# Attention plus swish-MLP on one core: feature order of heads 0 and 1 moved from the weight load into the PV copy and the norm, with a new instruction order

## The chip, the cores and the metric

The kernel runs on one core of one Trainium2 chip. The metric is the device time of one execution in microseconds (us); lower is better. Three timed runs of the kernel before gave 240.32, 236.54 and 239.46 us, so its median is 239.46 us. The execution that the profile shows took 237.53 us by the same clock, and the span of its instructions is 235.8 us. The engines are called as the profile calls them: PE is TensorE (PEld its weight load), DVE VectorE, ACT ScalarE, POOL GpSimd, SP SyncE, which here issues nearly all DMAs.

## The reference

Shapes: q, k and v are 4 batches x 8 heads x 768 positions x 64. Heads 0, 2 and 6 attend causally to everything ("retrieval"); the other five see the first 4 positions and a window of 64. The attention output, with the heads side by side as 512 features, is the input of a two-layer MLP with a swish of learned slope between the layers.

```python
scores = scale * np.matmul(q, k.transpose(0, 1, 3, 2))
full_mask = np.broadcast_to(causal, (H, S, S))
stream_mask = np.broadcast_to(causal & (is_sink | in_win), (H, S, S))
a = softmax(np.where(mask, scores, -1e9))
x = np.matmul(a, v).transpose(0, 2, 1, 3).reshape(B * S, H * D)   # 3072 x 512
h = x @ w_in                                                      # 512 x 2048
g = h * (1.0 / (1.0 + np.exp(-beta * h)))
out = g @ w_out                                                   # 2048 x 512
```

## The kernel before, in words

**Units.** The work is cut into 8 units n = 2b + u: batch b, half u of its sequence (384 query positions). A unit goes through these stages. `scores` (L624) makes keys-by-queries score tiles on PE; `exps` (L690) takes their exponential on ACT; `masks` (L699) multiplies by masks on DVE. `sums` or `sums_d` (L741, L766) add up the softmax denominators on PE. `pv` (L859) multiplies by v, four head pairs t = 0..3, two pairs to a PSUM tile (g = 0 and 1). The result is normalised into the bf16 tile xT, 128 features by 4 chunks by 384 positions. `mm1` (L919) multiplies xT by 16 feature tiles f of w_in, four matmuls each; `swish_a` (ACT) and `swish_b` (DVE) make gT; `mm2` (L936) multiplies gT by w_out; `out_copy` and `out_store` send it out.

**Two ways to normalise.** Units 0 and 1 copy the PV result to SBUF first (`hold`, L846), turn reciprocals on PE (`spread`) and multiply (`norm_held`, L851). Units 2 to 7 send the sums through DRAM to get a tile R with each head's reciprocals on its 64 partitions (`spread_r`, L812), and multiply PV by R straight out of PSUM (`norm`, L907).

**The order of the heads.** `XT` (L18) puts heads (1, 0) into chunk 0, so head 1 is on partitions 0 to 63 and head 0 on 64 to 127; the other chunks are natural: (2, 3), (4, 5), (6, 7). Thus the retrieval heads 0 and 2 of PV's first tile are on opposite halves of the partitions, and PE works on both halves side by side. xT keeps that order, so the first 128 rows of w_in have to be exchanged to match. `load_w0` (L483) does this as it loads them: four DMAs of 64 rows x 1024 columns (256 KB each) that land on the other half of the partitions. `cast_w0` (L505) turns them to bf16 in 8 pieces of 128 x 256. The other 384 rows come in four quarters of columns (`load_w_in`, L489: 128 x 3 x 512 numbers, 768 KB), each cast by POOL in four pieces of 128 x 3 x 128 (`cast_w_in`, L501). One such piece is the weight of one feature tile f. `XH` (L19) carries the exchanged order into the columns of the sums of units 0 and 1 (L367, L752).

**What sets the order.** Every operation is entered with `add`, with its needs and a planned cost. `_Plan.run` (L141) goes through them in the order of the list SEQUENCE (L37); where several engines could do an operation, CHOICE (L94) names one by a letter; the planned start times then give every engine its program order. Each engine's queue runs strictly in that order, SP's queue of DMA issues too. Staging tiles for the weights come from a ring of three (`wf`); each holds 8 KB per partition. At most 8 DMAs are under way: the issue of one waits for the landing of the eighth before it.

Of the kernel before, what the change touches and what calls it, by code (L numbers as in the profile page):

```python
# [8 lines left out]
F32 = mybir.dt.float32  # L9
# [9 lines left out]
XH = [h for t in XT for h in t]  # L19
RETR = [1, 0, 1, 0, 0, 0, 1, 0]  # L20
NQ = 384
# [71 lines left out]
]  # L93
CHOICE = (  # L94
    "daggaagdddgddaadadadgdgaaadgdddaagdgdaaaadadaaaddaddagdgadaadadggadgdgddadgdggggaadaadddaaaddaaddaaa"
    "dddddddda"
# [102 lines left out]
def kernel(  # L199
# [18 lines left out]
    NP = len(PAIRS)  # L218
# [138 lines left out]
    def const_sink():  # L357
# [6 lines left out]
        for pi in range(1, NP):  # L364
            for i, h in enumerate(PAIRS[pi]):
                if not RETR[h]:
                    c = XH.index(h)  # L367
                    dve.tensor_copy(out=esel_k[:, 16 + c:32:8], in_=sel_k[0:96, pi - 1, i:i + 1].to_broadcast([96, 2]))
                    dve.tensor_copy(out=sink_own[:, h:h + 1], in_=sel_k[0:96, pi - 1, i:i + 1])
# [113 lines left out]
    def load_w0(half, r):  # L483
        if (half, r) == (0, 0):
            wst["0"] = stg.tile([128, 2048], F32, name="wf", bufs=RINGS["wf"])
        c = slice(half * d_ff // 2, (half + 1) * d_ff // 2)
        sp.dma_start(out=wst["0"][r:r + D, c], in_=moe_w_in[D - r:2 * D - r, c])

    def load_w_in(s):  # L489
        f = stg.tile([128, 2048], F32, name="wf", bufs=RINGS["wf"])[:, 0:(NP - 1) * 2 * FS].rearrange("p (a n) -> p a n", a=NP - 1)  # L490
        sp.dma_start(out=f, in_=bass.AP(moe_w_in.tensor, moe_w_in.offset + 128 * d_ff + s * 2 * FS,
# [792 lines left out]
```

## Time and profile before

| | us |
|---|---|
| median of three runs (lowest, highest) | 239.46 (236.54, 240.32) |
| the profiled execution | 237.53 |
| span of its instructions | 235.8 |
| PE busy (share of the span) | 223.6 (95%) |
| DVE, ACT, POOL busy | 154.4, 139.0, 80.5 |
| mean granted clock of PE | 0.993 |

The views are read like this. The page gives busy time per engine and, in 40 slices, the busy tenths of each engine and PE's granted clock. The chain of waits follows back from the last instruction what each waited for. The timeline lists instructions in order of time, with the start, the time covered, and in brackets the idle time of the engine before them and what ended it. The groups by form have the count, the busy time and the mean duration of one.

### The profile page before, as it was taken

How to read it: one execution, taken by the hardware profiler on the slowest of the kernel's cores; microseconds unless marked ns; L12 is line 12 of the kernel's file. 1: busy time of each engine (PE TensorE's matmuls, PEld its weight loads, DVE VectorE, ACT ScalarE, POOL GpSimd, SP SyncE). 2: the span in 40 equal slices, each digit the busy share in tenths (PEclk: the TensorE clock that was granted, in tenths of full speed). 3: DMA queues.
4: the chain of work that ended last, by engine and by line, in shares of the span. 5: the costliest groups of instructions: out<-in, count | busy, mean ns of one | idle time of the engine just before them, and what ended most of it. 6: DMA issues, size and time to landing. Idle time of an engine off the chain costs nothing.

```text
span 235.8 us, 6232 instructions
## 1 busy us (share of the span) xinstructions
PE 223.6 (95%) x2462; PEld 126.1 (53%) x2462; DVE 154.4 (65%) x365; ACT 139.0 (59%) x236; POOL 80.5 (34%) x190
## 2 busy tenths in 40 slices
PE   7788599999999999999999999999999999999994
PEld 6454266665454555563655555554564465466553
DVE  6597479888727847882677588536777286258630
ACT  4898387888626639824886169613876267108600
POOL 5316356689564239609243145540000000000000
PEclk9999889999999999999999999999999999999999
DMA  6989979999988999999879978862600200703012
GB/s 185 275 256 321 238 185 313 361 369 291 227 214 210 198 189 250 238 202 254 215 178 236 238 167 224 166 155 97 133 3 29 107 2 10 179 0 133 3 44 89
DMA packets 84557, 42.37 MB, mean 180 GB/s; under 512 B 66592, under 2 KB 77552, under 8 KB 84528
## 3 DMA queue, kind: packets, MB, share of 16 engines
q1 hardware_dynamic: 84256, 41.78, 70.0%
q8 instruction: 19, 0.31, 0.5%
q10 hardware_dynamic: 272, 0.20, 0.3%
q14 instruction: 10, 0.08, 0.1%
HBM read 32.38 MB, written 6.37 MB: 164 GB/s over the span
## 4 chain that ended last, share of the span: by engine, by line
PE 85%; DMA 7%; DVE 5%; SPq 1%; ACT 1%; POOL 0%; issue 0%
PE b L115 74%; PE sp L115 10%; DMA wf<-in_moe_w_in_dram 5%; DVE es L115 2%; DMA k2f<-in_k_dram 2%; SPq L115 1%; DVE QK L115 1%; DVE vs L115 1%; POOL w_in L115 0%; DVE vb L115 0%; DVE c L115 0%; ACT t L115 0%; DVE gT L115 0%; DVE VE L115 0%; ACT es L115 0%
## 5 line engine op out<-in xcount | busy, mean ns | idle before, releaser
L115 PE MATMUL b<-xT,w_in 128*128 128x384 bf16 x512 | 91.1, 329 | 4.2 <-POOL w_in L115 4.1
L115 ACT ACTIVATE t<-b,beta_h 128x384 f32<-128x384 f32 x128 | 72.2, 583 | 34.2 <-PE b L115 23.1
L115 PE MATMUL b<-w_out,gT 128*128 128x512 bf16 (+1 forms) x400 | 88.8, 371 | 0.0
L115 DVE SCALAR_TENSOR_TENSOR gT<-t,b 128x384 bf16<-128x384 f32 x128 | 68.3, 551 | 27.6 <-ACT t L115 24.5
L115 PEld LDWEIGHTS <-w_in 128*128 128x128 bf16 x512 | 48.5, 98 | 38.7 <-POOL w_in L115 4.7
L115 ACT ACTIVATE es<-sp 128x768 bf16<-128x768 f32 (+3 forms) x64 | 49.9, 810 | 22.4 <-PE sp L115 21.9
L115 PEld LDWEIGHTS <-gT 128*128 128x128 bf16 x400 | 37.7, 98 | 39.8 <-issue 1.0
L115 POOL CAST c<-wf 128x256 bf16<-128x256 f32 x48 | 18.5, 422 | 22.2 <-DMA wf<-in_k_dram 10.6
L115 DVE TENSOR_SCALAR osb<-b 128x512 f32<-128x512 f32 (+1 forms) x15 | 9.9, 671 | 19.8 <-PE b L115 15.3
L115 PE MATMUL sp<-QK 64*64 64x64 bf16 (+6 forms) x402 | 18.9, 236 | 0.9 <-ACT QK L115 0.5
L115 ACT ACTIVATE osb<-b 128x512 f32<-128x512 f32 (+1 forms) x10 | 5.8, 577 | 22.9 <-PE b L115 22.8
L115 DVE TENSOR_TENSOR xT<-sp,R 128x768 bf16<-128x768 f32 (+3 forms) x18 | 11.6, 686 | 9.4 <-PE sp L115 9.4
L115 POOL COPY KP<-QK 128x64 bf16<-128x64 bf16 (+5 forms) x39 | 11.0, 332 | 18.0 <-DMA QK<-c 14.2
L115 PEld LDWEIGHTS <-QK 64*64 64x64 bf16 (+1 forms) x402 | 10.1, 106 | 11.6 <-issue 10.4
L115 DVE TENSOR_TENSOR es<-es,mask_s 128x800 bf16<-128x800 bf16 (+5 forms) x24 | 12.6, 537 | 3.9 <-ACT es L115 3.7
L115 POOL CAST vb<-wf 128x512 bf16<-128x512 f32 x18 | 10.7, 612 | 12.7 <-DMA wf<-in_v_dram 12.6
L115 POOL CAST w_in<-wf 128x384 bf16<-128x384 f32 (+1 forms) x20 | 9.6, 518 | 14.5 <-DMA wf<-in_moe_w_in_dram 14.5
L115 PE MATMUL sp<-es,vb 128*64 128x64 bf16 (+3 forms) x243 | 13.8, 237 | 0.0
L115 ACT COPY QK<-b 128x384 bf16<-128x384 bf16 (+1 forms) x15 | 8.8, 589 | 7.4 <-PE b L115 7.3
L115 PE MATMUL b<-ident,c 128*128 128x128 bf16 x96 | 9.8, 228 | 2.5 <-ACT c L115 0.9
L115 PEld LDWEIGHTS <-vb 128*64 128x64 bf16 x243 | 11.6, 111 | 0.5
L115 DVE TENSOR_TENSOR es<-es,mask_c 128x256 bf16<-128x256 bf16 (+2 forms) x32 | 10.7, 350 | 0.3 <-ACT es L115 0.2
(93 smaller groups left out, 170.7 us busy)
## 6 DMA issues: line engine op xcount, KB each, us to landing
out_dram<-osb SPq DMA_DIRECT2D x23, 256.0 KB
wf<-in_v_dram SPq DMA_DIRECT2D x18, 256.0 KB
wf<-in_moe_w_out_dram SPq DMA_DIRECT2D x4, 1024.0 KB
R<-rd SPq DMA_DIRECT2D x9, 384.0 KB
q2f<-in_q_dram SPq DMA_DIRECT2D x16, 192.0 KB
wf<-in_moe_w_in_dram SPq DMA_DIRECT2D x4, 768.0 KB
wf<-in_q_dram SPq DMA_DIRECT2D x12, 256.0 KB
wf<-in_k_dram SPq DMA_DIRECT2D x12, 256.0 KB
```

What stands on the lines that cost most here:

```text
L115: ins = f(*a, **k)
```

## The change

1. xT has the heads in natural order, so w_in is loaded plainly. `load_w0` and `cast_w0` go (4 DMAs, 8 casts); `load_w_in` loads all 512 rows of a quarter of the columns (128 x 4 x 512 numbers, 1024 KB), and its four casts on POOL have 512 numbers per partition where they had 384.
2. PV keeps heads (1, 0) in chunk 0 for units 1 to 7; unit 0 uses natural order there too. The exchange is made later: in unit 1 by `hold`, whose one copy of the first tile becomes three (64 x 384, 64 x 384, 128 x 384); in units 2 to 7 by `norm`, whose one multiplication of 128 x 768 for g = 0 becomes three of the same shapes. The halves cross partitions 0 to 63 and 64 to 127.
3. The sums of units 0 and 1 use the natural column h.
4. SEQUENCE and CHOICE are new, so the order on every engine is new, and some operations change engine: POOL does five of the eight shifts of v (`shift_v`) where it did two, output copies on DVE go from 15 to 9 (ACT from 10 to 16), casts of q and k on DVE and ACT go from 12 to 7, on POOL from 20 to 25.

```diff
-XH = [h for t in XT for h in t]
-                    c = XH.index(h)
+                    c = h
-    def load_w0(half, r):
-        if (half, r) == (0, 0):
-            wst["0"] = stg.tile([128, 2048], F32, name="wf", bufs=RINGS["wf"])
-        c = slice(half * d_ff // 2, (half + 1) * d_ff // 2)
-        sp.dma_start(out=wst["0"][r:r + D, c], in_=moe_w_in[D - r:2 * D - r, c])
     def load_w_in(s):
-        f = stg.tile([128, 2048], F32, name="wf", bufs=RINGS["wf"])[:, 0:(NP - 1) * 2 * FS].rearrange("p (a n) -> p a n", a=NP - 1)
+        f = stg.tile([128, 2048], F32, name="wf", bufs=RINGS["wf"]).rearrange("p (a n) -> p a n", a=NP)
...
-        cast(eng, w_in_sb[2 * s + i // 2][:, 1:, c], wst["i", s][:, :, i * 128:(i + 1) * 128])
-    def cast_w0(s, eng):
-        cast(eng, w_in_sb[s][:, 0, :], wst["0"][:, s * FS:(s + 1) * FS])
+        cast(eng, w_in_sb[2 * s + i // 2][:, :, c], wst["i", s][:, :, i * 128:(i + 1) * 128])
     def hold(x, g, eng):
-        cast(eng, x.R[:, 2 * g:2 * g + 2, :], x.ps.pop(("v", g))[:, :, 0:NQ])
+        o = x.ps.pop(("v", g))
+        if g or not x.n:
+            cast(eng, x.R[:, 2 * g:2 * g + 2, :], o[:, :, 0:NQ])
+            return
+        for r in (0, D):
+            cast(eng, x.R[r:r + D, 0, :], o[D - r:2 * D - r, 0, 0:NQ])
+        cast(eng, x.R[:, 1, :], o[:, 1, 0:NQ])
     def pv(x, g):
-            for i, h in enumerate(XT[t]):
+            for i, h in enumerate(XT[t] if x.n else (2 * t, 2 * t + 1)):
     def norm(x, g):
-        if not (g and moved(x, 6)):
+        if g == 0:
+            for r in (0, D):
+                dve.tensor_mul(x.xT[r:r + D, 0, :], o[D - r:2 * D - r, 0, 0:NQ], x.R[D - r:2 * D - r, 0, :])
+            dve.tensor_mul(x.xT[:, 1, :], o[:, 1, 0:NQ], x.R[:, 1, :])
+            return
+        if not moved(x, 6):
             dve.tensor_mul(x.xT[:, 2 * g:2 * g + 2, :], o[:, :, 0:NQ], x.R[:, 2 * g:2 * g + 2, :])
             return
```

**The new order around the weights.** In both kernels SP's 16th DMA is the first quarter of w_in. Behind it came, before: two pieces of `load_w0`, three loads of q and k (192 KB each), the second quarter, one load of q, the other two pieces, the third quarter, three loads of v. Now: four loads of q and k, the second quarter, the third quarter, three loads of v. On PE, six transposes and 14 score matmuls of unit 1 that stood behind f = 4 now stand ahead of it. After the PV of unit 7 PE now has 12 matmuls of `mm2` where it had 9 ahead of that unit's first `mm1`; after the PV of unit 5, 12 where it had 16 and 4 score matmuls.

More of the change, by code (lines that the diff above doesn't have):

```diff
@@ L37 @@
 SEQUENCE = [
[55 rows of a table removed]
[54 rows of a table added]
 ]
 CHOICE = (
-    "daggaagdddgddaadadadgdgaaadgdddaagdgdaaaadadaaaddaddagdgadaadadggadgdgddadgdggggaadaadddaaaddaaddaaa"
-    "dddddddda"
+    "ggggaaggdgdddadddadadggaagadggdaddggdaaddadaaaadgaddagagaddadagggdggaggdaggaadadaaaddaaadadaaadaadda"
+    "a"
 )
@@ L481 @@
     wst = {}
-    def load_w0(half, r):
-        if (half, r) == (0, 0):
-            wst["0"] = stg.tile([128, 2048], F32, name="wf", bufs=RINGS["wf"])
-        c = slice(half * d_ff // 2, (half + 1) * d_ff // 2)
-        sp.dma_start(out=wst["0"][r:r + D, c], in_=moe_w_in[D - r:2 * D - r, c])
     def load_w_in(s):
-        f = stg.tile([128, 2048], F32, name="wf", bufs=RINGS["wf"])[:, 0:(NP - 1) * 2 * FS].rearrange("p (a n) -> p a n", a=NP - 1)
-        sp.dma_start(out=f, in_=bass.AP(moe_w_in.tensor, moe_w_in.offset + 128 * d_ff + s * 2 * FS,
-                                        [[d_ff, 128], [128 * d_ff, NP - 1], [1, 2 * FS]]))
+        f = stg.tile([128, 2048], F32, name="wf", bufs=RINGS["wf"]).rearrange("p (a n) -> p a n", a=NP)
+        sp.dma_start(out=f, in_=bass.AP(moe_w_in.tensor, moe_w_in.offset + s * 2 * FS, [[d_ff, 128], [128 * d_ff, NP], [1, 2 * FS]]))
         wst["i", s] = f
@@ L751, in sums @@
                 for h in heads:
-                    e8 = two[:, 31 - 16 * s - XH.index(h):63 - 16 * s - XH.index(h)]
+                    e8 = two[:, 31 - 16 * s - h:63 - 16 * s - h]
                     if RETR[h]:
@@ L1145, in attention @@
             if n < RD:
-                add(("act", "dve"), (0.7, 0.87), lambda e, g=g: hold(x, g, ENG[e]),
+                add(("act", "dve"), (1.1, 1.4) if n and not g else (0.7, 0.87), lambda e, g=g: hold(x, g, ENG[e]),
                     needs=[("O", n, g)] + ([("o", n, 0)] if g else []), gives=[("o", n, g)], drop=[("sp", (n, "v", g))],
@@ L1149, in attention @@
                 continue
-            add("dve", 1.3 if u and g else 0.87, lambda g=g: norm(x, g),
+            add("dve", 0.87 if g and not u else 1.35, lambda g=g: norm(x, g),
                 needs=[("R", n, 2 * g), ("R", n, 2 * g + 1), ("o", n, g)] + ([("xT", n, 0)] if g else []),
@@ L1160, in first @@
         drop = [("xT", n)] if s == FO - 1 else []
-        needs = [("wi", s), ("w0", s // FO2)] + ([("h", n, s - 1)] if s else [])
+        needs = [("wi", s)] + ([("h", n, s - 1)] if s else [])
         if n == 0 and s < 2:
             for t in range(NP):
-                add("pe", 0.163, lambda t=t: mm1(x, s, [t]), needs=[("xT", n, t)] + ([("h", n, s, t - 1)] if t else needs if s != 1 else needs[:2] + [("h", n, 0, 0)]),
+                add("pe", 0.163, lambda t=t: mm1(x, s, [t]), needs=[("xT", n, t)] + ([("h", n, s, t - 1)] if t else needs if s != 1 else needs[:1] + [("h", n, 0, 0)]),
                     gives=[("h", n, s, t)] + ([("h", n, s)] if t == NP - 1 else []), take=[] if t else take)
@@ L1225 @@
     add("dve", 1.4, const_sel, needs=[("const", "ident")], gives=[("const", "sel")])
-    for half in range(2):
-        for r in (0, D):
-            first_one = (half, r) == (0, 0)
-            add("sp", 0.5, lambda half=half, r=r: load_w0(half, r), dma=0.72, gives=[("w0f", half, r)], begun=[("begun", "0")] if first_one else [],
-                needs=[] if first_one else [("begun", "0")], take=[("wf", "w0", NS)] if first_one else [])
-    for s in range(NS):
-        add(("pool", "dve", "act"), (0.36, 0.2, 0.33), lambda e, s=s: cast_w0(s, ENG[e]), port=True,
-            needs=[("w0f", s // 4, 0), ("w0f", s // 4, D)], gives=[("w0", s)], drop=[("wf", "w0")])
     for s in range(NS // 2):
         for w, ld, ca in (("i", load_w_in, cast_w_in), ("o", load_w_out, cast_w_out)):
-            add("sp", 0.5, lambda s=s, ld=ld: ld(s), dma=2.9 if w == "o" else 2.2, gives=[("wf", w, s)], begun=[("begun", w, s)],
+            add("sp", 0.5, lambda s=s, ld=ld: ld(s), dma=2.9, gives=[("wf", w, s)], begun=[("begun", w, s)],
                 take=[("wf", (w, s), 4)])
             for i in range(4):
-                add("pool", 0.58 if w == "o" else 0.47, lambda s=s, i=i, ca=ca: ca(s, i, pool), needs=[("wf", w, s)],
+                add("pool", 0.58, lambda s=s, i=i, ca=ca: ca(s, i, pool), needs=[("wf", w, s)],
                     gives=[("w" + w, 4 * s + i)], drop=[("wf", (w, s))])
```

109 rows, old and new, of the table SEQUENCE are left out of this document.

## The prediction

> **What bounds the kernel now.** I read the page first: busy times, then slices and granted clock.
>
> ```profile
> PE 223.6 (95%) x2462; PEld 126.1 (53%) x2462; DVE 154.4 (65%) x365; ACT 139.0 (59%) x236; POOL 80.5 (34%) x190
> ...
> PE   7788599999999999999999999999999999999994
> ...
> PEclk9999889999999999999999999999999999999999
> ```
>
> PE is the bound, and it is full from the sixth slice (about 30 us) on. No other engine passes 65%. The windows say the same in numbers:
>
> ```profile
> 20.00:30.00 10.00, 6.43 (x63) 3.52 (x64) 5.37 (x13) 5.29 (x10) 4.63 (x10) 0.90 1.08 290
> 30.00:40.00 10.00, 10.00 (x229) 6.55 (x226) 8.21 (x19) 7.74 (x15) 5.31 (x11) 0.93 0.82 234
> 40.00:90.00 50.00, 49.55 (x537) 26.90 (x532) 35.33 (x86) 32.56 (x53) 30.85 (x69) 1.00 1.00 258
> 90.00:150.00 60.00, 60.00 (x684) 32.89 (x681) 43.01 (x100) 39.23 (x68) 29.28 (x64) 1.00 0.95 218
> 150.00:210.00 60.00, 60.00 (x573) 32.49 (x572) 34.26 (x71) 28.90 (x50) 2.87 (x10) 1.00 0.32 80
> ```
>
> From 30 to 210 us PE idles 0.45 us in all. So whatever does not change PE's own work (matmuls go from 2462 to 2463, one more filler) can gain only ahead of 30 us, and can lose anywhere. Ahead of 30 us the largest hole is in this stretch of PE's timeline, with the clock of the stretches behind it:
>
> ```profile
> 23.55 1.64 PE L115 MATMUL b<-xT,w_in 128*128 128x384 bf16 x9
> 28.12 1.14 PE L115 MATMUL b<-xT,w_in 128*128 128x384 bf16 x3 [2.93 <-POOL w_in L115]
> 29.05 0.53 PE L115 MATMUL b<-ident,c 128*128 128x128 bf16 x3
> 29.51 0.53 PE L115 MATMUL sp<-QK 64*64 64x64 bf16 x14
> 29.98 0.50 PE L115 MATMUL b<-ident,c 128*128 128x128 bf16 x3
> 30.27 2.05 PE L115 MATMUL b<-xT,w_in 128*128 128x384 bf16 x8
> 32.25 0.36 PE L115 MATMUL sp<-QK 64*64 64x64 bf16 x14
> 32.55 1.47 PE L115 MATMUL b<-xT,w_in 128*128 128x384 bf16 x8
> ```
>
> ```profile
> 28.00:30.00 2.00, 1.88 (x21) 1.06 (x22) 2.00 (x5) 0.58 (x1) 1.21 (x3) 0.51 1.15 302
> 30.00:32.00 2.00, 2.00 (x15) 1.18 (x11) 1.80 (x6) 1.48 (x3) 0.26 (x1) 0.64 0.48 115
> ```
>
> After f = 3 PE has nothing for 2.93 us, until POOL has cast the second quarter of w_in. Then it runs at a granted clock of 0.51 and 0.64 for four microseconds: 2 x 0.49 + 2 x 0.36 = 1.7 us lost. The hole costs 2.9 + 1.7 = 4.6 us in all. POOL's rows and the chain say that a DMA is behind it:
>
> ```profile
> 17.77 1.41 POOL L115 CAST w_in<-wf 128x384 bf16<-128x384 f32 x3 [5.06 <-DMA wf<-in_moe_w_in_dram]
> ...
> 27.10 2.11 POOL L115 CAST w_in<-wf 128x384 bf16<-128x384 f32 x4 [4.40 <-DMA wf<-in_moe_w_in_dram]
> 31.75 1.41 POOL L115 CAST w_in<-wf 128x384 bf16<-128x384 f32 x3 [2.54 <-DMA wf<-in_moe_w_in_dram]
> ```
>
> ```profile
> 16.28 10.77 DMA wf<-in_moe_w_in_dram
> ```
>
> The quarter was issued at 16.28 and landed 10.77 us later. DMA engines were busy all that time (share 1.08 in the window 20 to 30), so bytes set its time: what stands ahead of it in SP's queue decides.
>
> **The change, part by part.**
>
> *Bytes ahead of the second quarter.* Between the casts at 17.77 and 27.10 there landed, by the code's sizes and SP's order, 2 x 256 + 3 x 192 + 768 = 1856 KB in 9.33 us, or 199 KB/us. Up to the end of the second quarter the new order has 256 KB more in the first, 512 KB of `load_w0` less, 192 KB of q or k more and 256 KB more in the second: 192 KB more. At 199 KB/us that is 0.96 us later; at the 290 GB/s of the whole window 0.68. I take 0.8, so it lands at 27.9. It is now SP's 21st DMA where it was the 22nd, so I give the limit of eight DMAs under way nothing; the full DMA engines cover that.
>
> *The casts.* One cast of 128 x 384 becomes 128 x 512; the nearest row is w_out's cast of that shape:
>
> ```profile
> L115 POOL CAST w_out<-wf 128x512 bf16<-128x512 f32 x16 | 9.2, 616 | 1.9 <-DMA wf<-in_moe_w_out_dram 1.9
> ...
> L115 POOL CAST w_in<-wf 128x384 bf16<-128x384 f32 x16 | 8.0, 536 | 13.5 <-DMA wf<-in_moe_w_in_dram 13.5
> L115 POOL CAST w_in<-wf 128x256 bf16<-128x256 f32 x4 | 1.7, 446 | 1.0 <-DMA wf<-in_moe_w_in_dram 1.0
> ```
>
> 16 x 0.08 = 1.3 us more on POOL against 4 x 0.446 = 1.8 us less there, and four pieces less on ACT and DVE. In the new POOL order f = 4's piece is cast first, where it was second: f = 4 starts at 27.9 + 0.62 + 0.05 = 28.6, 0.45 us later than now. f = 5's piece is third, at 27.9 + 3 x 0.62 = 29.8; at half clock f = 4 lasts until 28.6 + 1.3 = 29.9, which hides it.
>
> *Work moved into the hole.* Six transposes and 14 score matmuls now run behind f = 4, from 29.05 to 30.27 at half clock: 1.2 us. The new order does them ahead of f = 4, in the hole, where they cost nothing. Net at this place: 0.45 - 1.2 = -0.8 us. If PE could not do them there (their loads of q and k now stand ahead of the second quarter, so I expect that it can), the place would cost +0.45.
>
> *The third quarter.* Up to its end there are now 256 KB fewer, about 1 us: cast from 30.7 instead of 31.75. PE comes to f = 8 at about 33, as now (32.55 + 0.7). Hidden. It costs from the point where it lands after 32.5.
>
> *The exchange in the norm.* Durations on DVE by form:
>
> ```profile
> L115 DVE TENSOR_TENSOR xT<-sp,R 128x768 bf16<-128x768 f32 x9 | 8.3, 953 | 9.4 <-PE sp L115 9.4
> ...
> L115 DVE TENSOR_TENSOR xT<-sp,R 128x384 bf16<-128x384 f32 x3 | 1.6, 548 | 0.0
> ...
> L115 DVE TENSOR_TENSOR xT<-sp,R 64x128 bf16<-64x128 f32 x3 | 0.9, 294 | 0.0
> ```
>
> No row has 64 x 384. From below it is 0.294 (64 x 128), from above 0.548 (128 x 384); I take 0.548, since the length per partition is the same. Each of six norms is then 3 x 0.548 - 0.953 = 0.69 us longer, 4.1 us on DVE in all, and 0 at the lower end. DVE is at 65% and loses work elsewhere (seven of 21 copies of shifted v, six of 15 output copies), so only the place counts: PE's first `mm1` of the unit waits for xT. The tightest place now is unit 7:
>
> ```profile
> 209.08 2.06 DVE L115 TENSOR_TENSOR xT<-sp,R 128x768 bf16<-128x768 f32 x4 [1.99 <-PE sp L115]
> 211.18 0.29 DVE L115 TENSOR_TENSOR xT<-sp,q2f 64x128 bf16<-64x128 f32 x1
> ```
>
> ```profile
> 209.72 2.12 PE L115 MATMUL b<-w_out,gT 128*128 128x512 bf16 x9
> 211.68 2.60 PE L115 MATMUL b<-xT,w_in 128*128 128x384 bf16 x15
> ```
>
> DVE ends at 211.47, PE needs xT at 211.68. Nine `mm2` matmuls cover the norm, 0.218 each; the new order has twelve, so PE comes to `mm1` at 209.72 + 2.62 = 212.3, and DVE ends at 211.47 + 0.69 = 212.2. I cost it at nothing; the cover is 0.1 to 0.2 us there, and any other DVE work ahead of it ends the cover.
>
> *The exchange in `hold`* (unit 1) is one copy of 0.8 us that becomes three of about 0.48, 0.65 us more on ACT, at about 40 us:
>
> ```profile
> L115 ACT COPY QK<-b 128x384 bf16<-128x384 bf16 x10 | 4.8, 484 | 0.1
> ...
> L115 ACT COPY R<-sp 128x768 f32<-128x768 f32 x4 | 3.2, 799 | 0.7 <-PE sp L115 0.6
> ```
>
> PE now has three `mm1` tiles between the spreads there, 2 us, so I take 0; exposed it would be 0.65. PV of unit 0 has both retrieval heads on one half now; at PE's rate that is under 0.1 us, taken as 0.1. Shifted v on POOL (five units, not two) takes some 3 us of POOL per unit; at 34% POOL hides it.
>
> *Sum.* -0.8 + 0.1 = -0.7 us. The profiled execution (237.53, of which 1.7 us lie outside its span of 235.8) would go to 236.8. It was 1.9 us below the median of the runs, 239.46, and I put the same step on the median: **238.8 us**.
>
> [...] In the rows, a hole of 2.93 us was followed by a granted clock of about one half. [...]
>
> **The rivals.**
> - A, as above: 238.8, of its own 236.4 to 240.9, since three runs of one kernel already spread from 236.54 to 240.32. Chance 0.42.
> - B, the hole gets shorter by the moved work, and the clock is never halved: 1.7 us less, 237.1. For it: 1.2 us of work at half clock is 0.7 us at full, out of 2.93. Against it: the quarter lands later. Chance 0.15.
> - F, the hole closes: DMAs of full 128 rows flow faster than 199 KB/us and the second quarter lands by 25 us: 4.6 + 0.8 us less, 234.0. Against it: the DMA engines' share is already 1.08. Chance 0.10.
> - C, the other side: xT comes late. DVE takes the norm after other work in its queue, and the 0.69 us shows in all six units, with hold's 0.65: 4.1 + 0.65 = 4.8 us, 239.5 + 4.8 = 244.2. It decides from 0.2 us of DVE work ahead of the norm. For it: DVE is busy 35.33 of 50 us between 40 and 90. Against it: the twelve matmuls of cover. Chance 0.18.
> - D, a second hole: three loads deep in the queue, f = 8 waits for the third quarter as f = 4 does for the second, and the clock halves again: 4.6 us, 243.4. Against it: fewer bytes ahead. Chance 0.15.
>
> That the change does nothing (239.5) lies within A.
>
> **How the numbers follow.** The time is A's. The range reaches to F on one side and C on the other, 235.0 to 243.8, leaving out some 0.2. A difference under 2% (4.8 us) is about what a measurement of this kernel cannot tell from none. Faster by over 2%: F, 0.10. Slower by over 2%: most of C and D where they come with a late run, 0.22. Within 2%: 0.68.
>
> **What would show it.** Right: a hole before f = 4 of about 2.9 us that ends near 28.6, with transposes and scores ahead of it and a half clock behind it; no hole at f = 8; no PE wait for xT after 60 us; about 0.5 us of idle PE from 30 us on. Wrong: a second wait for POOL's w_in, waits of PE for DVE's xT of 0.3 us or more in several units, or more filler or stalls in the first 20 us than now.

## The result and the profile after

| | before | after |
|---|---|---|
| median of 20 runs (lowest, highest), us | 236.14 (233.98, 240.32) | 234.26 (231.85, 238.26) |
| profiled execution, its span, us | 237.53, 235.8 | 235.09, 233.4 |
| mean granted clock in that execution | 0.993 | 1.0 |

The ratio of after to before is 0.9922, 95% interval 0.9893 to 0.9951: the kernel became 0.8% faster, 1.9 us. Here and below medians are of all runs of a kernel, while ratios, their intervals and means leave out the runs that lay over 1.5% above the kernel's fastest. The prediction was 238.8 with 235.0 to 243.8, so the measured 234.26 lies below its range. Most of the difference to 238.8 is the base: the three runs shown had a median of 239.46, twenty runs have 236.14. The change itself was put at -0.7 us and measured -1.9.

The page of after: busy time, then PE's slices and clock.

```profile
PE 222.8 (95%) x2443; PEld 126.8 (54%) x2463; DVE 160.1 (69%) x357; ACT 141.7 (61%) x238; POOL 95.9 (41%) x202
...
PE   6999999998999899999999999999999999999994
...
PEclk9999999999999999999999999999999999999999
```

The fifth slice was a 5 and is a 9, and the clock never drops; further right two slices are now an 8. In windows (columns: length, then busy time of PE, PEld, DVE, ACT and POOL, granted clock, DMA share, GB/s):

```profile
20.00:30.00 10.00, 9.40 (x101) 5.09 (x100) 8.96 (x18) 8.38 (x15) 7.51 (x13) 1.00 0.98 296
30.00:40.00 10.00, 10.00 (x221) 6.89 (x220) 9.26 (x22) 7.48 (x15) 5.99 (x13) 1.00 1.02 341
...
50.00:60.00 10.00, 8.78 (x118) 4.38 (x112) 9.41 (x24) 5.81 (x10) 9.66 (x17) 1.00 0.87 231
70.00:80.00 10.00, 9.47 (x167) 4.88 (x168) 7.37 (x16) 5.15 (x7) 8.07 (x13) 1.00 0.97 238
80.00:90.00 10.00, 9.26 (x73) 5.51 (x74) 8.62 (x19) 6.11 (x11) 2.79 (x11) 1.00 0.80 162
```

From 20 to 30 us PE was busy 6.43 us and is busy 9.40, at full clock. But behind 50 us it now loses time. (Twenty matmul records are missing from this trace, 2443 of 2463. They leave gaps of 0.05 or 0.16 us that are put down to "issue", some 1.7 us in all; those are not waits.) PE's timeline of after names the waits, and POOL's shows when the weights came:

```profile
24.14 0.33 PE L113 MATMUL b<-ident,c 128*128 128x128 bf16 x3
24.41 0.36 PE L113 MATMUL sp<-QK 64*64 64x64 bf16 x14
24.70 0.34 PE L113 MATMUL b<-ident,c 128*128 128x128 bf16 x3
25.14 0.82 PE L113 MATMUL b<-xT,w_in 128*128 128x384 bf16 x4
26.25 0.82 PE L113 MATMUL b<-xT,w_in 128*128 128x384 bf16 x4 [0.29 <-POOL w_in L113]
...
56.57 2.53 PE L113 MATMUL b<-w_out,gT 128*128 128x512 bf16 x11 [0.92 <-POOL w_out L113]
...
80.58 1.09 PE L113 MATMUL b<-es,one 128*32 128x384 bf16 x25 [0.90 <-DVE es L113]
```

```profile
18.47 2.42 POOL L113 CAST w_in<-wf 128x512 bf16<-128x512 f32 x4 [6.47 <-DMA wf<-in_moe_w_in_dram]
24.46 4.28 POOL L113 CAST w_in<-wf 128x512 bf16<-128x512 f32 x7 [2.49 <-DMA wf<-in_moe_w_in_dram]
...
49.74 6.77 POOL L113 CAST w_out<-wf 128x512 bf16<-128x512 f32 x11 [1.83 <-DMA wf<-in_moe_w_out_dram]
...
76.51 3.30 POOL L113 COPY vs<-vb 64x1536 bf16<-64x1536 bf16 x2
```

The second quarter is cast at 24.46 us instead of 27.10, though 192 KB more have to land by its end. The moved transposes and scores run before f = 4 (24.14 to 25.1), f = 4 starts at 25.14, f = 5 waits 0.29 us, and the hole of 2.93 us is gone with the half clock behind it. Counted by its `mm1` matmuls, PE comes to f = 8 at 28.89 us instead of 33.21, 4.3 us sooner. Of this, 1.4 us it already has at f = 0 (19.22 instead of 20.64), ahead of the hole: in the first 20 us PE idled 5.0 us before and idles 2.8 after. The span is only 2.4 us shorter. Most of the rest went back in waits that before did not have: 0.92 for a cast of w_out, 0.90 for a mask on DVE, and small ones.

These two waits differ between executions. In a second profile of the changed kernel (span 232.5; it is the last run on the exchange, below) the one for w_out is absent, and the one for the mask is twice as long:

```profile
79.53 1.09 PE L113 MATMUL b<-es,one 128*32 128x384 bf16 x25 [1.80 <-DVE es L113]
```

### The profile page after: what moved, and what is told of

Its sections match the earlier page's. It is cut to its first block, busy times and chain, and to the rows that moved or that the text cites. A ratio compares the mean times of both kernels' runs of the same rounds, so it can differ in the third digit from the quotient of the medians.

```text
span 233.4 us, 6215 instructions
## 1 busy us (share of the span) xinstructions
PE 222.8 (95%) x2443; PEld 126.8 (54%) x2463; DVE 160.1 (69%) x357; ACT 141.7 (61%) x238; POOL 95.9 (41%) x202
## 4 chain that ended last, share of the span: by engine, by line
PE 78%; DVE 8%; ACT 5%; DMA 4%; issue 2%; POOL 2%; SPq 0%; POOLq 0%; ACTq 0%
PE b L113 69%; PE sp L113 9%; DVE es L113 4%; DMA wf<-in_moe_w_in_dram 4%; ACT es L113 3%; DVE gT L113 2%; DVE mask_s L113 1%; DVE xT L113 1%; POOL w_in L113 1%; ACT t L113 1%; ACT QK L113 1%; POOL mask_s L113 1%; ACT c L113 0%; POOL ident L113 0%; POOL mask_c L113 0%
## 5 line engine op out<-in xcount | busy, mean ns | idle before, releaser
L113 PE MATMUL b<-w_out,gT 128*128 128x512 bf16 (+1 forms) x380 | 86.3, 370 | 2.9 <-issue 1.1
L113 ACT ACTIVATE es<-sp 128x768 bf16<-128x768 f32 (+2 forms) x64 | 49.2, 804 | 9.4 <-PE sp L113 9.3
L113 ACT ACTIVATE osb<-b 128x512 f32<-128x512 f32 (+1 forms) x16 | 9.1, 572 | 35.3 <-PE b L113 35.3
L113 DVE TENSOR_TENSOR xT<-sp,R 64x384 bf16<-64x384 f32 (+4 forms) x30 | 15.9, 554 | 11.4 <-PE sp L113 11.0
L113 DVE TENSOR_TENSOR es<-es,mask_c 128x256 bf16<-128x256 bf16 (+2 forms) x32 | 14.1, 454 | 12.3 <-ACT es L113 12.1
L113 DVE TENSOR_TENSOR es<-es,mask_s 128x800 bf16<-128x800 bf16 (+5 forms) x24 | 16.1, 692 | 0.8 <-ACT es L113 0.8
L113 POOL COPY vs<-vb 64x1536 bf16<-64x1536 bf16 (+2 forms) x12 | 15.7, 1321 | 0.3
L113 POOL CAST w_in<-wf 128x512 bf16<-128x512 f32 x16 | 9.7, 649 | 12.2 <-DMA wf<-in_moe_w_in_dram 12.2
L113 ACT COPY QK<-b 128x384 bf16<-128x384 bf16 (+1 forms) x12 | 7.1, 590 | 7.2 <-PE b L113 7.0
L113 DVE COPY QK<-b 128x384 bf16<-128x384 bf16 (+1 forms) x12 | 7.9, 685 | 5.0 <-PE b L113 5.0
```

The costliest lines, as they stand in the source:

```text
L113: ins = f(*a, **k)
```

## The experiments

Two theories for the early quarter. P: the `load_w0` DMAs themselves were slow, because each fills 64 of the 128 partitions. O: the new order (what stands ahead of the quarter, and PE's order) did it. A third question is who gave part of the gain back: the exchange on DVE, or the new order.

### Loads alone, in the old order

The kernel before, with the plain quarters and without `load_w0` and `cast_w0`; the exchange is left out, so the rows of w_in for heads 0 and 1 are not matched to xT.

```diff
-        sp.dma_start(out=wst["0"][r:r + D, c], in_=moe_w_in[D - r:2 * D - r, c])
+        pass
...
-        f = stg.tile([128, 2048], F32, name="wf", bufs=RINGS["wf"])[:, 0:(NP - 1) * 2 * FS].rearrange("p (a n) -> p a n", a=NP - 1)
+        f = stg.tile([128, 2048], F32, name="wf", bufs=RINGS["wf"]).rearrange("p (a n) -> p a n", a=NP)
...
-        cast(eng, w_in_sb[s][:, 0, :], wst["0"][:, s * FS:(s + 1) * FS])
+        pass
```

> The kernel before with its own order; only the four loads of 64 rows of w_in and their casts are left out, and the four quarters bring all 512 rows (heads 0 and 1 then meet each other's rows of w_in, which is left so). Theory P (the 64-row loads are slow for their bytes and hold up the second quarter): the second quarter lands by about 24.5 to 25.5 us instead of 27.1, the wait of 2.93 us before f = 4 falls under 1 us, the clock is not halved, and the span goes from 235.8 to 231 to 232 us, ratio 0.98. Theory O (the new order closed the hole: work moved ahead of f = 4, SP's order): only bytes count, which are 320 KB fewer up to that quarter, about 1.2 us; a wait of 1.5 to 2.5 us stays, ratio 0.99 to 1.00.

Measured: 232.63 us, ratio to before 0.9839 (0.9787 to 0.9892). POOL's timeline:

```profile
22.32 2.53 POOL L115 CAST w_in<-wf 128x512 bf16<-128x512 f32 x4 [2.32 <-DMA wf<-in_moe_w_in_dram]
```

Up to the end of the second quarter this kernel loads exactly as many bytes as before (256 KB more in each of two quarters, 512 KB of `load_w0` less; the 320 KB fewer of the expectation were a slip), in the same order, and has them 4.8 us sooner. Neither bytes nor the new order can be the cause of that, so O falls. What is left is the shape of the DMAs, or their number, which is two less up to there; the next two runs tell these apart. The loads alone gain 1.6%, twice what the whole change gains.

The 4.8 us compare one execution with one, and part of them is chance. A load lands in 16 parts, each with an event of its own in the trace, and the cast waits for the last. The parts of the second quarter landed at 22.39 (first), 23.29 (median), 24.81 (fifteenth) and 27.05 us (last) in the profile before, and at 20.61, 20.98, 21.29 and 22.27 in this one. So 2.3 us lie in the median part; the rest is a longer tail, mostly one late part. In all the profiles here the last part of this quarter comes 0.1 to 2.2 us behind the fifteenth, whatever the shape; what makes it late is not shown.

### Only the shape of load_w0

Both keep the bytes, the places in the queue and `cast_w0`, and leave the exchange out. The first has four DMAs of 128 rows x 512 columns, the second two of 128 x 1024 (the same 4 KB runs as before, on 128 partitions).

```diff
+        c0 = half * d_ff // 2 + r // D * d_ff // 4
+        c = slice(c0, c0 + d_ff // 4)
+        sp.dma_start(out=wst["0"][:, c], in_=moe_w_in[0:128, c])
```

```diff
+        if r == 0:
+            sp.dma_start(out=wst["0"][:, c], in_=moe_w_in[0:128, c])
```

> The kernel before with the same four DMAs of 256 KB at the same places, each of 128 rows x 512 columns instead of 64 rows x 1024 columns (the exchange of heads 0 and 1 is thereby left out). Theory P: the shape is the cause, so the second quarter lands 1.5 to 2.5 us sooner and the ratio is 0.985 to 0.99. Theory O, or bytes alone: no difference, the quarter lands at 27 us and the ratio is 1.00.

> The kernel before with the first 128 rows in two DMAs of 128 rows x 1024 columns (512 KB each; the exchange of heads 0 and 1 is left out), so that the packets stay 4 KB long but reach all 128 partitions. If half the partitions are what makes the 64-row loads slow: like e2, the quarter lands 1.5 to 2.5 us sooner. If packets of 4 KB are: like the kernel before, 27 us.

Measured: 0.9888 (0.9854 to 0.9922) and 0.9893 (0.9857 to 0.993). The two agree, so 2 KB or 4 KB runs, and four DMAs or two, make no difference; 64 or 128 partitions make 1.1%. Theory P holds. The quarter is cast at, in the first and in the second:

```profile
25.84 2.11 POOL L115 CAST w_in<-wf 128x384 bf16<-128x384 f32 x4 [2.63 <-DMA wf<-in_moe_w_in_dram]
```

```profile
24.14 2.11 POOL L115 CAST w_in<-wf 128x384 bf16<-128x384 f32 x4 [2.41 <-DMA wf<-in_moe_w_in_dram]
```

That is 1.3 and 3.0 us sooner than before's 27.10, but the first is no sooner than the second profile of before, below (25.87). (The profiled execution of the first took 236.88 us, against a median of 233.79, and its last part came 1.6 us behind the fifteenth.) A measure that does not hang on a late part: from the median part of the first quarter to that of the third, the bytes that SP's order has there (3328 KB before, in 12.33 us) go at 270 KB/us in the profile before, and at 243 in its second one below. With `load_w0` on 128 partitions they go at 323 and 339, with plain quarters at 375 to 387 (five profiles: loads alone twice, loads with the exchange, the changed kernel twice). With 64-row pieces in the changed kernel, the next experiment, it is 295.

### The converse: 64-row pieces in the kernel after

The changed kernel with the first 128 rows of each quarter loaded in two pieces of 64 rows.

```diff
-        sp.dma_start(out=f, in_=bass.AP(moe_w_in.tensor, moe_w_in.offset + s * 2 * FS, [[d_ff, 128], [128 * d_ff, NP], [1, 2 * FS]]))
+        sp.dma_start(out=f[:, 1:, :], in_=bass.AP(moe_w_in.tensor, moe_w_in.offset + 128 * d_ff + s * 2 * FS, [[d_ff, 128], [128 * d_ff, NP - 1], [1, 2 * FS]]))
+        for r in (0, D):
+            sp.dma_start(out=f[r:r + D, 0, :], in_=moe_w_in[r:r + D, s * 2 * FS:(s + 1) * 2 * FS])
```

> The changed kernel, but each quarter of w_in comes as one DMA of 128 x 3 x 512 and two of 64 x 512 for the first 128 rows (same bytes, rows in natural order, 8 more DMAs). Theory P (loads on 64 partitions are slow): the second quarter is cast later than 24.46 us, by 0.5 to 2 us, and the kernel loses some 0.5%, 0.995 to 1.0 of the kernel before. Rival L (only the 4 KB packets, or the two pieces that stood ahead of the second quarter, were slow): no difference to the changed kernel, 0.99 to 0.993.

Measured: 1.0016 (0.9977 to 1.0055) of before; the changed kernel beside it on the same chip had 0.9894 (0.9845 to 0.9943). The whole gain is gone. (One of its twelve executions took 566.3 us, for a reason that nothing here shows.) POOL's timeline, and PE's waits (total, times, longest):

```profile
26.51 2.61 POOL L113 CAST w_in<-wf 128x512 bf16<-128x512 f32 x4 [3.23 <-DMA wf<-in_moe_w_in_dram]
```

```profile
PE b L113 <- POOL w_in L113: 3.0, 4, 1.2
```

Same bytes, 2.05 us later than after's 24.46, and PE waits four times for w_in, 3.0 us in all. Eight DMAs more are a second difference that this run does not separate; the runs before it, which add none, do. Its span, 237.1, is 3.7 us longer than that of the profile after, and some 2.7 us of this are waits for w_in.

### The kernel before once more

No edit; one execution.

> The kernel before once more, for a second profile. If the late second quarter belongs to the kernel: it is cast at 26 to 28 us again, with a wait of PE of 2 to 3 us before f = 4. If it was an accident of one execution: cast by 25 us, wait under 1 us.

It took 240.0 us. POOL's and PE's timelines, and two windows of the clock:

```profile
19.43 1.41 POOL L115 CAST w_in<-wf 128x384 bf16<-128x384 f32 x3 [8.13 <-DMA wf<-in_moe_w_in_dram]
...
25.87 1.86 POOL L115 CAST w_in<-wf 128x384 bf16<-128x384 f32 x4 [1.67 <-DMA wf<-in_moe_w_in_dram]
```

```profile
21.95 0.82 PE L115 MATMUL b<-xT,w_in 128*128 128x384 bf16 x2 [3.86 <-POOL w_in L115]
```

```profile
22.00:24.00 2.00, 2.00 (x14) 0.86 (x15) 1.83 (x4) 0.65 (x1) 2.00 (x5) 0.50 1.10 322
24.00:26.00 2.00, 2.00 (x12) 1.10 (x12) 0.36 (x1) 1.27 (x4) 0.33 (x2) 0.50 1.03 220
```

Here the first quarter was the late one, and the hole, 3.86 us, came ahead of f = 1. The half clock behind it lasted from about 21 to 31 us though PE was busy all the time from 22 us on, and cost some 4.7 us, more than the hole. So both profiles of the kernel before have a hole for late weights, and its place varies. The mean granted clock of a run is a weaker sign: it was under 0.995 in 42 of 56 runs of before beside the experiments and in three of 26 of after, but also in 16 of 25 of the two kernels with `load_w0` on 128 partitions. It goes with the old order too: with plain loads it was under 0.995 in 7 of 18 runs in the old order and in 4 of 55 in the new.

### Does the exchange cost?

First the changed kernel without the exchange in `hold` and `norm` (part of the computation left out: features of heads 0 and 1 stand exchanged against w_in):

```diff
-            for r in (0, D):
-                dve.tensor_mul(x.xT[r:r + D, 0, :], o[D - r:2 * D - r, 0, 0:NQ], x.R[D - r:2 * D - r, 0, :])
-            dve.tensor_mul(x.xT[:, 1, :], o[:, 1, 0:NQ], x.R[:, 1, :])
+            dve.tensor_mul(x.xT[:, 0:2, :], o[:, :, 0:NQ], x.R[:, 0:2, :])
```

> The changed kernel with the exchange of heads 0 and 1 left out of the norm and of hold (one multiplication of 128 x 768 instead of three, one copy instead of three). Theory X (the exchange is what gives part of the gain back): DVE has 4 us less work, waits of PE after 50 us shrink from about 2 to about 1 us, ratio to the kernel before 0.985 against 0.992 for the changed kernel. My own reading (the waits at 55.7 and 79.7 us come from POOL's casts of w_out and from masks on DVE that run beside POOL's copies): the ratio stays at 0.991 to 0.993.

Measured: 0.9877 (0.9828 to 0.9925) against 0.9922 (0.9893 to 0.9951) with it. That is outside the 0.991 to 0.993 expected, but the intervals overlap. So three more on one chip: the loads alone again, the same with the exchange (the change's code in the old order of instructions), and the changed kernel again.

```diff
-        cast(eng, x.R[:, 2 * g:2 * g + 2, :], x.ps.pop(("v", g))[:, :, 0:NQ])
+        for r in (0, D):
+            cast(eng, x.R[r:r + D, 0, :], o[D - r:2 * D - r, 0, 0:NQ])
+        cast(eng, x.R[:, 1, :], o[:, 1, 0:NQ])
...
-            for i, h in enumerate(XT[t]):
+            for i, h in enumerate(XT[t] if x.n else (2 * t, 2 * t + 1)):
...
+            for r in (0, D):
+                dve.tensor_mul(x.xT[r:r + D, 0, :], o[D - r:2 * D - r, 0, 0:NQ], x.R[D - r:2 * D - r, 0, :])
```

> The same as the kernel before with plain quarters and no exchange at all (rows of w_in of heads 0 and 1 left as they come), once more, beside the kernel with the exchange on the same chip. Expected 0.982 to 0.986 as in the first run (0.9839). The difference to the kernel with the exchange is the price of the exchange in the old order: P+N expects 0 to 0.4%, rival X 0.8% or more.

> The changed kernel's code (plain quarters, natural order in the features, exchange in hold and norm) in the old order of instructions. Theory P+N: the plain loads give 1.6% (0.9839 with the exchange left out), the exchange itself costs little (0 to 1 us), and what the change gives back comes from the new order (shifted v on POOL beside the masks, casts of w_out, 2 us of PE waits after 50 us). Then this runs at 0.984 to 0.988 of the kernel before, faster than the changed kernel (0.992). Rival X: the exchange costs the 4 us of longer work on DVE in the old order too, so 0.992 or above. In the profile P+N expects the second quarter cast by 23 us, no PE wait above 1 us after 20 us and no half clock.

> The changed kernel once more, on the same chip: 0.990 to 0.995. The difference to the same code in the old order is the price of the new order: P+N expects 0.4 to 0.8%, rival X none.

| kernel | us | ratio to before |
|---|---|---|
| loads alone, old order | 232.72 | 0.9832 (0.9775 to 0.9888) |
| loads and exchange, old order | 234.48 | 0.986 (0.98 to 0.992) |
| loads, exchange and new order (after) | 234.33 | 0.9894 (0.9845 to 0.9943) |

From the first row to the last the means differ by 1.5 us (0.7 to 2.3, by drawing the five runs of each anew), so exchange and new order together do cost. Each step alone does not stand out: exchange 0.7 us (-0.5 to 2.0), new order 0.8 us (-0.4 to 1.9). The profile speaks against a large price of the exchange. Windows of loads-and-exchange in the old order:

```profile
14.00:16.00 2.00, 2.00 (x53) 1.39 (x52) 1.68 (x6) 2.00 (x5) 0.00 (x0) 0.50 0.90 319
16.00:18.00 2.00, 2.00 (x47) 1.73 (x47) 1.76 (x6) 0.93 (x2) 0.28 (x1) 0.71 1.06 381
...
60.00:100.00 40.00, 39.87 (x486) 21.77 (x484) 28.10 (x70) 23.47 (x37) 19.99 (x45) 1.00 0.98 215
100.00:150.00 50.00, 49.95 (x504) 26.15 (x503) 34.84 (x83) 29.97 (x51) 21.22 (x47) 1.00 0.97 203
150.00:210.00 60.00, 59.94 (x573) 32.72 (x572) 37.34 (x80) 28.19 (x49) 2.47 (x9) 1.00 0.29 71
```

In the 150 us in which six units are normalised, PE idles 0.24 us. This execution's span was 232.0, 1.0 more than that of the loads alone in the run beside it (231.0; 230.1 in the first), and it lost time to a halved clock early on (2 x 0.50 + 2 x 0.29 = 1.6 us). So the cost of the exchange is argued to be small, not shown.

### Two waits of the new order

What are the 0.90 and the 0.92 us? In the first, POOL copies shifted v (76.51, 3.30 us) while DVE multiplies masks. One letter of CHOICE puts that unit's copies on DVE:

```diff
+        choice.update({242: 'd'})
```

> The changed kernel with one letter: unit 3's shift of v is done by DVE instead of POOL. Theory G (DVE's masks slow down beside POOL's copies, 3.88 us for three of 128 x 816 where 0.58 us each is usual): those masks return to about 0.6 us each, the wait of PE for DVE's es before the sums of unit 3 (0.90 us at 79.7 us) goes, and the time falls by 0.8 us, ratio to the kernel before 0.988. Rival (DVE is simply late): its own copies of 1.2 us come on top, and the wait stays or grows; ratio 0.992 to 0.995.

DVE's timeline of after, then of this kernel (a group of three masks, two of 816 numbers and one of 408, named after the first); then the groups by form of after and of this kernel (mean ns of one behind the busy time):

```profile
76.65 3.88 DVE L113 TENSOR_TENSOR es<-es,mask_s 128x816 bf16<-128x816 bf16 x3
```

```profile
79.65 1.34 DVE L113 TENSOR_TENSOR es<-es,mask_s 128x816 bf16<-128x816 bf16 x3
```

```profile
L113 DVE TENSOR_TENSOR es<-es,mask_s 128x816 bf16<-128x816 bf16 x6 | 4.7, 787 | 0.2 <-ACT es L113 0.2
...
L113 DVE TENSOR_TENSOR es<-es,mask_s 128x408 bf16<-128x408 bf16 x3 | 2.4, 786 | 0.0
```

```profile
L113 DVE TENSOR_TENSOR es<-es,mask_s 128x816 bf16<-128x816 bf16 x6 | 3.4, 575 | 0.2 <-ACT es L113 0.2
...
L113 DVE TENSOR_TENSOR es<-es,mask_s 128x408 bf16<-128x408 bf16 x3 | 1.1, 362 | 0.0
```

The three masks take 3.88 us beside POOL's copies and 1.34 without. By the means, 6 x (787 - 575) and 3 x (786 - 362) ns, one mask of each length was 1.27 us longer: 1.84 and 1.63 us instead of 0.57 and 0.36. The third lies behind the copies and is not longer. The wait of 0.90 is gone. Casts on POOL do the same: a mask of 128 x 512 just ahead of these three, with POOL's casts of q, k and v beside it back to back, took 1.74 us in the changed kernel, 1.68 in this one and 2.64 in the second profile of after, where a like mask with nothing on POOL takes 0.42. The 0.90 us between 1.74 and 2.64 are the difference between the waits of 0.90 and 1.80. In time: 233.7, ratio 0.9879 (0.9829 to 0.9928), the interval overlapping after's 0.9922 (0.9893 to 0.9951). The price is 2.5 us of DVE for 3.3 us of copies. That the masks return to their usual time when the copies leave POOL, this run shows; why, no run here does.

The other wait: the eleven casts at 49.74 begin with pieces of two quarters of w_out, whose casts stand in the order 504, 513, 515, 505, 514, 503, 516, 506 (numbers of operations; 503 to 506 are the quarter that lands first). Three pieces that have landed by 45.63 us so wait behind 513, whose quarter landed at 49.69 (its median part at 46.62: again one late part). In landing order:

```diff
+        first = [503, 504, 505, 506, 513, 514, 515, 516]
+        places = [i for i, o in enumerate(SEQUENCE) if o in first]
+        for i, o in zip(places, first):
+            SEQUENCE[i] = o
```

> The changed kernel with the eight casts of w_out's first and second quarter in the order in which they land, instead of mixed. Three more pieces are then cast in POOL's idle time from 47.9 to 49.7 us, so the last pieces are ready 1.8 us sooner and the wait of PE of 0.92 us at 55.7 us goes: 0.9 us less, ratio to the kernel before 0.988. Rival (the fourth quarter's landing at 53.3 us sets that wait): no difference.

> Both edits of the two kernels before this one. If the two waits are independent: 1.7 us less than the changed kernel, ratio to the kernel before 0.984 to 0.985. If one delay only uncovers the next: 0.988 to 0.990.

Alone: 234.1, ratio 0.991 (0.9871 to 0.9948), no different from after. The 0.92 is gone (as it is in the second profile of after, without the edit), and other waits stay or come out; PE's timeline:

```profile
79.70 1.09 PE L113 MATMUL b<-es,one 128*32 128x384 bf16 x25 [1.13 <-DVE es L113]
...
137.05 0.22 PE L113 MATMUL sp<-QK,KP 64*64 64x64 bf16 x2 [0.75 <-DVE KP L113]
139.22 0.97 PE L113 MATMUL b<-xT,w_in 128*128 128x384 bf16 x5 [0.40 <-DVE gT L113]
```

Both edits together: 233.28, ratio 0.986 (0.9813 to 0.9907), profiled span 231.5. Neither wait is there, and what is left is small:

```profile
86.48 2.76 PE L113 MATMUL b<-xT,w_in 128*128 128x384 bf16 x16 [0.62 <-DVE gT L113]
95.84 0.85 PE L113 MATMUL b<-w_out,gT 128*128 128x512 bf16 x3 [0.35 <-DVE gT L113]
97.33 1.24 PE L113 MATMUL b<-w_out,gT 128*128 128x512 bf16 x5 [0.63 <-DVE gT L113]
```

This kernel beats before, and in its point estimate after by 0.6%, with intervals that overlap. It is as fast as the change's code in the old order (0.986, 0.98 to 0.992): these runs show no gain in time from the new order, not even with both waits gone.

## Why the prediction was right or wrong, point by point

- **What bounds the kernel: right in the main.** PE was the bound from 30 us on, and the largest thing to win was the hole ahead of f = 4. "Can lose anywhere" was right too. The first 20 us, where PE idled 5.0 us, had no term in the sum; 1.4 us came from there.
- **"Bytes ahead of the second quarter": the step that failed.** It took 199 KB/us as the rate of the DMA engines, whatever they carried, because their share was 1.08, and so made more bytes a later quarter. A share says how long the engines were busy, not how well they were used: from 20 to 30 us it was 1.08 with 290 GB/s before and is 0.98 with 296 after. Two things were wrong. First, loads of different shape flow at different rates: 243 to 295 KB/us with 64-row pieces among them, 323 to 387 without (the measure of the experiments). Second, the stretch of 9.33 us ends with the last of 16 parts, which was 2.2 us late; from median part to median part the same 1856 KB took 6.22 us, 298 KB/us, near the 290 GB/s of the window. So the quarter came 3.4 us before the 27.9 predicted (24.46), with more bytes. Of the 2.6 us by which it came sooner than before, 0.6 us are in its median part (22.67 instead of 23.29); the other 2.0 us are that its last part was less late. So the two profiles alone would not show the cause; the run times of the experiments do.

  In the packets of before, the 4 KB packets of `load_w0` took 284 ns at the median, 71 per KB, and the 2 KB packets of the w_in quarters 84 ns, 42 per KB. The same 4 KB packets on 128 partitions took 159 ns, 40 per KB. The 71 and the 42 ns per KB are in the trace of before; weighed beside the 199 KB/us, they speak for F.
- **Rivals.** F ("the hole closes", 234.0, chance 0.10) named the right mechanism, and B's full clock came with it. F's price for the hole, 4.6 us, was about right (2.6 of 2.93 us and the half clock's 1.7 are gone in the two profiles), but it was set on a base 3.3 us too high and gave nothing back. That its 234.0 is so near the 234.26 is therefore luck. C and D did not occur.
- **The casts: right.** 16 casts of 128 x 512 take 649 ns each; taken 616.
- **PV of unit 0, +0.1: right**, though no row stood behind it. Its 44 matmuls cover 1.73 us instead of 1.61.
- **Work moved into the hole: half right.** It runs ahead of f = 4 as said; with no hole left it covers the wait instead of filling a longer one.
- **Third quarter hidden: right.** Its casts follow without a wait of PE.
- **The exchange in the norm: right in size and cover.** 64 x 384 was put at 0.548 us:

```profile
L113 DVE TENSOR_TENSOR xT<-sp,R 64x384 bf16<-64x384 f32 x12 | 6.7, 555 | 11.2 <-PE sp L113 11.0
```

  For unit 7 the cover was put at 0.1 to 0.2 us; DVE's and PE's timelines of after:

```profile
206.09 2.83 DVE L113 TENSOR_TENSOR xT<-sp,R 64x384 bf16<-64x384 f32 x6 [3.44 <-PE sp L113]
208.95 0.29 DVE L113 TENSOR_TENSOR xT<-sp,q2f 64x128 bf16<-64x128 f32 x1
```

```profile
209.33 6.99 PE L113 MATMUL b<-xT,w_in 128*128 128x384 bf16 x42
```

  DVE ends at 209.24, PE starts at 209.33 without a wait. What the exchange costs in time stays open within -0.5 to 2.0 us.
- **"At 34% POOL hides it" (shifted v on POOL): wrong.** POOL had the time, but its two copies made two of DVE's masks 1.3 us longer each, and PE waited 0.90 us. Free time on POOL did not make work on it free for DVE.
- **About 0.5 us of idle PE behind 30 us: wrong.** After has some 2.4 us without the gaps of missing records, and 2.5 in its second profile; the waits for w_out's casts and for the masks had no term.
- **The base.** The step was put on the median of three runs, 239.46, while the profiled execution, 237.53, from which it was worked out, lay nearer to the 236.14 of twenty.

What stays open: how the 1.5 us that exchange and new order cost together divide between them, and why one part of a load comes late.

## What to carry to other kernels

Do not divide bytes by time across DMAs of different shapes: price each shape from rows of its own, look whether one late part made the stretch long, and be wary of a DMA on 64 partitions even when the DMA engines look busy (here 71 ns per KB against 40 on 128 partitions, at a share of 1.08). When a stall at the start goes, look at what the time saved runs into, since here about 2 of 4.3 us went into waits that the old stall had covered or the new order made. Before moving copies or casts to an idle POOL, look at which DVE instructions run at that time: here two masks took 1.84 and 1.63 us instead of 0.57 and 0.36.

## What the runs showed of the hardware that was not expected

- The DMAs into 64 partitions were slow for their bytes: their 4 KB packets took 71 ns per KB against 40 on 128 partitions, and the same bytes on 128 partitions made the whole kernel 1.1% faster (0.9893, 0.9857 to 0.993).
- Beside POOL copies of 1.65 us each, two of DVE's two-input bf16 masks took 1.84 and 1.63 us instead of 0.57 and 0.36.
- The clock was halved in six of the profiles, and the length of the hole before it does not tell when. It came behind holes of PE of 2.93 and 3.86 us (both profiles of before), but also behind 1.54 us (`load_w0` as 128 x 512, 0.51 from 30 to 32 us) and 1.33 us (the copies of unit 3 on DVE, 0.50 from 22 to 28 us). It came also with no hole over 0.5 us in the ten microseconds before: in the windows of loads-and-exchange above and in the run of `load_w0` as 128 x 1024 (0.50 from 16 to 18 us). A wait of 1.80 us in a run of after left it full. What halves it, no run here shows.
